# Moving the decode of most token mixing weights later, and centring the gate's rows on ScalarE

## The chip, the cores and the metric

One core of a Trainium2 chip. The metric is the device time of one execution in microseconds, as the median of several runs; the profile is of one further execution. The core's engines are TensorE (PE), VectorE (DVE), ScalarE (ACT), GpSimd (POOL) and SyncE (SP), each of which works through its own instructions in a fixed order and waits in that order; transfers are issued from SP's and GpSimd's queues.

## What is computed

Three layers follow one another, with a batch of 4, 768 tokens, 8 heads of 48 and a width of 384:

```python
f = 1.0 / (1.0 + np.exp(-f_logit))
for t in range(S):
    state = f[:, :, t, :, None] * state + np.einsum('bhd,bhe->bhde', k[:, :, t], v[:, :, t])
    y[:, :, t] = np.einsum('bhd,bhde->bhe', q[:, :, t], state)
...
u, v = (h[..., :d_ff // 2], h[..., d_ff // 2:])    # h = gelu(x @ w_in)
v_n = (v - mu) / np.sqrt(var + 1e-06) * g_ln
v_s = np.einsum('ts,bsd->btd', w_sg, v_n) + b_sg[None, :, None]
x = x + (u * v_s) @ w_out
...
zr, zi = x * np.cos(x @ w_theta), x * np.sin(x @ w_theta)
u = x + np.einsum('ts,bsd->btd', w_tok_r, zr) + np.einsum('ts,bsd->btd', w_tok_i, zi)
out = u + np.maximum(u @ w_ch, 0.0)
```

`v - mu` is the centring of the gate's rows; `w_tok_r` and `w_tok_i` are the token mixing weights. Weights come as 64-bit floats.

## The kernel before, in words

Every product is made of three matmuls (L782 to L784) from operands split into a high and a low part. A planner (`Plan`, L172) holds each operation with an engine, a duration, what it reads and writes, and a due time `vt`. It runs through time once, on each engine takes the ready operation with the earliest due time (pulled earlier where a reader's due time asks for it), and so writes one fixed order for each engine. What a due time does depends on the buffers too: an operation whose buffer is held is not ready.

The work comes in this order. Attention of batch 0 runs alone. Then block1 (L932, the second layer) of batches 0 to 3, each with attention of the next batch spread over it (24 attention units in all; each transposes keys, updates states and multiplies), so that the block1 of batch 3, the last, has none beside it. Then block2 (L968 and on, the third layer) of batch 3, then of 0, 1 and 2. In block1 each of six chunks of 128 tokens is multiplied by the gate's half of `w_in`, goes through Gelu on ScalarE with a row sum (L957), is centred on VectorE (L963 scales the sum to minus the mean, L964 adds it), squared with a row sum (L969), and scaled by GpSimd's power of the variance (L981, L989). `p3` (L831) mixes over tokens in two passes of 72 matmuls; each pass ends with the evacuation of four accumulations (L845, L850, then hi cast L791 and low half L792). `p4` adds the output product; the one of the second pass of tokens is left over for the block that follows. In block2, `theta` (L867) makes the cosines and sines for six chunks, then `p6` (L902) streams 24 tiles of mixing weights.

Each mixing tile (24 of 128x384) is decoded once and kept in DRAM: `load_f32` (L411) loads the raw 64-bit words on SP's queue, ScalarE takes a first pass (L431), VectorE four of bit work (L432 to L435); `load_split` (L437) adds the hi cast on ScalarE (L445) and the low half on VectorE (L446) into a buffer `wt`, and `decode` (L477) writes `wt` to DRAM on GpSimd's queue (L482). There are two `raw`, three `dt` and one `wt` buffer. `stream` (L484) reads the tiles back into five `st` buffers on SP's queue. `channel_weights` (L460) does the same for `w_theta` and `w_ch` in chunks, into `wmid`; `channel_load` (L470) brings them back into the place of `w_in`. Due times of decodes are set at the end of `body`, where `va` is the end of block1 of batch 0 and `pl.vt` that of block1 of batch 3, in the planner's time.

Of the kernel before, what the change touches and what calls it, by code (L numbers as in the profile page):

```python
# [12 lines left out]
AF = mybir.ActivationFunctionType  # L13
# [36 lines left out]
N_W = 1  # L50
N_DT = 3
N_RAW = 2
BG_FROM = 0.0
BG_TO = 80.0
N_MM = 4
GROUPS0 = [(p, p + 1) for p in range(NP)]
GROUPS1 = GROUPS0
# [265 lines left out]
def body(tc, ctx, att, qkv, flog, w_in, g_ln, w_sgT, b_sg, w_out, w_theta, w_rT, w_iT, w_ch, out):  # L323
# [84 lines left out]
    def a1(n):  # L408
        return 0.1 + n * 0.00081
# [67 lines left out]
    def decode(pl, g, i, vt):  # L477
        m, s, t = order[i]
        w = pl.buf(g.w32, [P, 2, TH], F32R)
        src = srcs[m][s * P : (s + 1) * P, t * TH : (t + 1) * TH]  # L480
        load_split(pl, g, w, lambda: (w.t[:, 0], w.t[:, 1]), src, vt, background=True)
        dma(pl, "POOL", P * 3072, lambda: nc.gpsimd.dma_start(scratch1[i], w.t.bitcast(F32)), [w], [g.scr1[i]], vt=vt)  # L482
# [105 lines left out]
    def unit(pl, g, b, hf, p, f, fb, seed, sb, be, bb, t, parts, xst, carry):  # L588
# [84 lines left out]
        def state(c):  # L673
            (s0, b0), (s1, b1) = S[c], S[c + 1]
            if hf == 0 and c == 0:
                pl.op("DVE", 0.117, lambda: V.tensor_copy(s1(), U(0)), r=[ps], w=[b1])
            elif c % 2 or c == 0:
                b1 = fulls[c // 2] if c % 2 else b1
                s1 = (lambda: st.t[:, 2 * NC2 + c // 2]) if c % 2 else s1
                pl.op("DVE", 0.117, lambda: V.tensor_add(s1(), s0(), U(c)), r=[ps, b0], w=[b1])  # L680
            else:
                be_ = be[:, c // 2 - 1 : c // 2]
                pl.op(
                    "DVE", 0.117,
                    lambda: V.scalar_tensor_tensor(s1(), st.t[:, 2 * NC2 + c // 2 - 1], be_, U(c), ALU.mult, ALU.add), r=[ps, fulls[c // 2 - 1], bb], w=[b1],  # L685
                )
            if c % 2:
                s2, b2 = S[c + 1]
                pl.op(
                    "ACT", 0.23, lambda: nc.scalar.activation(s2(), s1(), AF.Copy, scale=be[:, c // 2 : c // 2 + 1]), r=[bb, fulls[c // 2]], w=[b2]  # L690
                )
# [77 lines left out]
    def moe(pl, g, xst, get, wmid, out_b, pace, first=False):  # L769
# [162 lines left out]
        def block1(before, resplit, keep=None):  # L932
            xsplits((0,) if first else (0, 1))
            stat = pl.buf(g.stat, [P, 3, NS])
            sm, sv, sr = ([Buf(of=stat) for _ in range(NS)] for _ in range(3))
            vn = [pl.buf(g.ar[i], [P, 2, 3, DH], F32R) for i in range(2)]
            vnb = [[Buf(of=vn[s // 3]) for _ in range(2)] for s in range(NS)]
            vts = []

            def vtiles(s, c=slice(None)):  # L940
                return vnb[s], lambda: (vn[s // 3].t[:, 0, s % 3, c], vn[s // 3].t[:, 1, s % 3, c])

            for s in range(NS):
                if s == NC2:
                    before()
                    if first:
                        u0 = p2(0)
                        xsplits((1,))
                ps = pl.buf(g.mm, [P, 512])
                hf, c = s // NC2, slice((s % NC2) * P, (s % NC2 + 1) * P)  # L950
                for k in range(NK):
                    w = g.win[k][2:]
                    mm3(ps, xtiles(hf, k, c), (w, lambda k=k: (win[:, 0, k, DH:], win[:, 1, k, DH:])), k == 0, k == NK - 1, DH)
                vt = pl.buf(g.tmp, [P, DH])
                pl.op(
                    "ACT", a1(DH) + 0.05,
                    lambda ps=ps, vt=vt, s=s: A(vt.t, ps.t, AF.Gelu_apprx_tanh, accum_out=stat.t[:, 0, s : s + 1]),  # L957
                    [ps], [vt, sm[s]], table="G",
                )

                def centre(vt=vt, s=s):
                    m = stat.t[:, 0, s : s + 1]
                    V.tensor_scalar(m, m, -1.0 / DH, None, ALU.mult)  # L963
                    V.tensor_scalar(vt.t, vt.t, m, None, ALU.add)  # L964

                pl.op("DVE", 0.5, centre, [], [vt, sm[s]])
                pl.op(
                    "ACT", a1(DH) + 0.1,  # L968
                    lambda vt=vt, s=s: A(junk, vt.t, AF.Square, accum_out=stat.t[:, 1, s : s + 1]), [vt], [sv[s]],  # L969
                )  # L970
                vts.append(vt)
                if s % 3 == 2:
                    gs = slice(s - 2, s + 1)
                    pl.op(
                        "DVE", 0.07,
                        lambda gs=gs: V.tensor_scalar(stat.t[:, 2, gs], stat.t[:, 1, gs], 1.0 / DH, 1e-6, ALU.mult, ALU.add),
                        sv[gs], sr[gs],
                    )
                    pl.op(
                        "POOL", 0.8,  # L980
                        lambda gs=gs: nc.gpsimd.tensor_tensor(stat.t[:, 2, gs], stat.t[:, 2, gs], mhalf[:, gs], ALU.pow),  # L981
                        [], sr[gs],
                    )
                    for i in range(s - 2, s + 1):
                        hi, lo = vnb[i]
                        tl = vtiles(i)[1]
                        pl.op(
                            "ACT", a1(DH) + 0.1,
                            lambda i=i, tl=tl: nc.scalar.mul(tl()[0], vts[i].t, stat.t[:, 2, i : i + 1]), [vts[i], sr[i]], [hi],  # L989
                        )  # L990
                        pl.op(
                            "DVE", v1(DH),
                            lambda i=i, tl=tl: V.scalar_tensor_tensor(
                                tl()[1], vts[i].t, stat.t[:, 2, i : i + 1], tl()[0].bitcast(F32), ALU.mult, ALU.subtract
                            ),
                            [vts[i], sr[i], hi], [lo],
                        )

            if not first:
                u0 = p2(0)  # L1000
            g0 = p3(0, u0, vtiles)
            if first:
                weights_out(pl, g, pl.vt)
            u1 = p2(1)
            p4(0, g0, resplit, keep)
            g1 = p3(1, u1, vtiles)
            return lambda: p4(1, g1, resplit, keep)
# [26 lines left out]
    with tc.manual_schedule():  # L1034
# [27 lines left out]
        for b in range(B):  # L1062
# [5 lines left out]
                va = pl.vt  # L1068
            if b != last:
                x = spread(b + 1, v + (pl.vt - v) * (LATE / 100 if b == 0 else 0.0))  # L1070
        n = len(order) - 2 * NS
        for i in range(n):
            if i in (n // 3, 2 * n // 3):
                channel_weights(pl, g, i // (n // 3) - 1, va + (pl.vt - va) * (BG_FROM + (BG_TO - BG_FROM) * i / n) / 100)
            decode(pl, g, 2 * NS + i, va + (pl.vt - va) * (BG_FROM + (BG_TO - BG_FROM) * i / n) / 100)
        mids = [channel_load(pl, g, i, pl.vt - 8.0, i) for i in range(2)]
        for b in (last, *range(last)):
            if b != last:
                x = []
# [157 lines left out]
```

## Time and profile before

| what | value |
|---|---|
| median of 3 runs | 677.27 us (672.85 to 678.81) |
| the profiled execution's own time | 677.74 us |
| its span, first to last instruction | 676.0 us |
| mean granted TensorE clock | 0.975 |
| busy TensorE, VectorE | 616.3, 453.6 us |
| busy ScalarE, GpSimd | 342.3, 99.5 us |

Busy time is time in which at least one instruction of an engine runs. Matmuls overlap, so that a busy TensorE need not be at its peak; its granted clock is given as a share of the full 2.4 GHz.

### The profile page before, as it was taken

Reading aid. Unit: us, or ns where it says so; the run is one execution under the profiler, and the core shown is the slowest. Engines: PE = TensorE matmul, PEld = TensorE weight load, DVE = VectorE, ACT = ScalarE, POOL = GpSimd, SP = SyncE. Lnnn points to the kernel's source line nnn. Section 1 sums busy time; section 2 is a strip of 40 time slices with the busy share of each in tenths; the row PEclk is TensorE's granted clock in tenths of the full one; section 3 lists DMA queues with packets and bytes.
Section 4 is the critical chain, followed back from the end, with each engine's and each line's share of the span. In section 5 each row is a group of like instructions: output and inputs, shape, how many; then the busy total and the mean of one; then the engine's idle time right before and its main releaser. Section 6 shows DMA issues by size and latency. Waiting matters only on the chain.

```text
span 676.0 us, 15027 instructions
## 1 busy us (share of the span) xinstructions
PE 616.3 (91%) x5953; PEld 569.8 (84%) x5953; DVE 453.6 (67%) x1077; ACT 342.3 (51%) x728; POOL 99.5 (15%) x178
## 2 busy tenths in 40 slices
PE   8788688989999988988989999899999999999996
PEld 8667567778788876878878999799989998998995
DVE  6999778969999897889979333741482175148203
ACT  6658587646685665675536421740291055019200
POOL 2000222143241340341131100000000000000000
PEclk9899969999999998999999999999999999999998
DMA  9522836377578787477575455058628844860762
GB/s 331 190 84 74 285 120 217 120 264 270 170 252 248 245 258 270 147 245 250 173 264 212 144 190 182 23 165 253 207 77 277 252 154 156 252 219 25 250 194 76
DMA packets 49296, 131.50 MB, mean 195 GB/s; under 512 B 6816, under 2 KB 17248, under 8 KB 48960
## 3 DMA queue, kind: packets, MB, share of 16 engines
q1 hardware_dynamic: 38656, 88.95, 41.2%
q0 software_dynamic: 10560, 41.49, 17.7%
q8 instruction: 49, 0.80, 0.5%
q14 instruction: 31, 0.25, 0.1%
HBM read 100.93 MB, written 24.77 MB: 186 GB/s over the span
## 4 chain that ended last, share of the span: by engine, by line
PE 42%; DVE 23%; ACT 11%; DMA 11%; issue 9%; POOL 2%; SPq 0%; DVEq 0%; POOLq 0%; ACTq 0%
PE mm L782 14%; PE mm L783 13%; PE mm L784 13%; DMA f<-in_flog 3%; DMA scratch<-wt 3%; DMA dt<-in_w_sgT 2%; DMA raw<-in_w_iT 2%; DVE s L680 2%; DVE dt L434 1%; DVE dt L435 1%; ACT ar L791 1%; DVE s L685 1%; DVE am L660 1%; POOL xst L755 1%; DVE tmp L845 1%
## 5 line engine op out<-in xcount | busy, mean ns | idle before, releaser
L782 PE MATMUL mm<-st,ar 128*128 128x384 f32 x480 | 164.9, 344 | 2.5 <-DMA st<-scratch 2.4
L783 PE MATMUL mm<-st,ar 128*128 128x384 f32 x480 | 161.4, 336 | 0.0
L784 PE MATMUL mm<-st,ar 128*128 128x384 f32 x480 | 161.4, 336 | 0.0
L801 ACT CAST x<-xst 128x384 fp32r<-128x384 f32 x72 | 36.9, 513 | 146.8 <-DVE xst L806 126.7
L806 DVE TENSOR_TENSOR xst<-xst,mm 128x384 f32<-128x384 f32 x48 | 25.7, 552 | 115.4 <-PE mm L784 115.4
L782 PEld LDWEIGHTS mm<-st,ar 128*128 128x128 f32 x480 | 90.9, 189 | 5.1 <-DMA st<-scratch 2.7
L783 PEld LDWEIGHTS mm<-st,ar 128*128 128x128 f32 x480 | 91.0, 190 | 0.1
L784 PEld LDWEIGHTS mm<-st,ar 128*128 128x128 f32 x480 | 90.8, 189 | 0.0
L782 PE MATMUL mm<-win,x 128*128 128x512 f32 (+1 forms) x144 | 56.6, 393 | 7.4 <-DVE tmp L845 3.7
L782 PE MATMUL mm<-x,win 128*128 128x384 f32 x168 | 58.4, 348 | 0.0
L784 PE MATMUL mm<-win,x 128*128 128x512 f32 (+1 forms) x144 | 54.1, 376 | 3.0 <-DVE x L802 3.0
L791 ACT CAST ar<-tmp 128x384 fp32r<-128x384 f32 x80 | 37.7, 509 | 37.7 <-DVE tmp L850 36.8
L784 PE MATMUL mm<-x,win 128*128 128x384 f32 x168 | 56.3, 335 | 0.0
L783 PE MATMUL mm<-x,win 128*128 128x384 f32 x168 | 56.2, 335 | 0.0
L783 PE MATMUL mm<-win,x 128*128 128x512 f32 (+1 forms) x144 | 53.5, 372 | 0.1
L802 DVE TENSOR_TENSOR x<-xst,x 128x384 fp32r<-128x384 f32 x72 | 37.8, 553 | 7.7 <-ACT x L801 6.4
L792 DVE TENSOR_TENSOR ar<-tmp,ar 128x384 fp32r<-128x384 f32 x80 | 41.0, 553 | 0.7 <-ACT ar L791 0.2
L782 PE MATMUL mm<-ar,wout 128*128 128x384 f32 x96 | 35.6, 371 | 4.2 <-DVE tmp L845 2.4
L782 PEld LDWEIGHTS mm<-win,x 128*128 128x128 f32 x144 | 27.8, 193 | 13.1 <-DVE tmp L845 5.4
L784 PE MATMUL mm<-ar,wout 128*128 128x384 f32 x96 | 33.3, 347 | 1.1 <-DVE wout L446 1.1
L755 POOL DMA_DIRECT2D xst<-y x60 | 30.7, 516 | 20.8 <-ACT y L732 10.9
L783 PE MATMUL mm<-ar,wout 128*128 128x384 f32 x96 | 33.4, 348 | 0.4 <-DVE ar L792 0.4
(146 smaller groups left out, 1227.2 us busy)
## 6 DMA issues: line engine op xcount, KB each, us to landing
st<-scratch SPq DMA_DIRECT2D x132, 384.0 KB, 3.8
qkv<-in_qkv POOLq DMA_DIRECT2D x24, 536.0 KB, 6.1
scratch<-wt POOLq DMA_DIRECT2D x24, 384.0 KB, 4.1
raw<-in_w_rT SPq DMA_DIRECT2D x12, 384.0 KB, 5.7
raw<-in_w_iT SPq DMA_DIRECT2D x12, 384.0 KB, 3.9
f<-in_flog POOLq DMA_DIRECT2D x6, 768.0 KB, 4.8
scratch<-st POOLq DMA_DIRECT2D x12, 384.0 KB, 6.7
out<-xst SPq DMA_DIRECT2D x24, 192.0 KB, 2.0
```

The lines of the kernel that those rows point to most:

```text
L434: op(v1(n), lambda: V.scalar_tensor_tensor(iget(), bits()[1], -0x40000000, iget(), ALU.bitwise_and, ALU.bitwise_or))
L435: op(v1(n), lambda: V.scalar_tensor_tensor(iget(), bits()[0], 29, iget(), ALU.logical_shift_right, ALU.bitwise_or))
L680: pl.op("DVE", 0.117, lambda: V.tensor_add(s1(), s0(), U(c)), r=[ps, b0], w=[b1])
L755: lambda r0=r0, n=n, kc=kc, o=64 * j + off: q[yq].dma_start(xst.t[r0 : r0 + n, kc], y.t[o : o + n].rearrange("p i a t -> p (i a t)")),
L782: nc.tensor.matmul(o, h0, h1, start=start, stop=False)
L783: nc.tensor.matmul(o, h0, l1, start=False, stop=False)
L784: nc.tensor.matmul(o, l0, h1, start=False, stop=stop)
L791: pl.op("ACT", a1(n), lambda: nc.scalar.copy(tiles()[0], src.t[:, :n]), [src], [hi])
L792: pl.op("DVE", v1(n), lambda: V.tensor_sub(tiles()[1], src.t[:, :n], tiles()[0].bitcast(F32)), [src, hi], [lo])
L801: pl.op("ACT", a1(TH), lambda: nc.scalar.copy(X[hf][:, 0, k], T()), [src], [hi])
L802: pl.op("DVE", v1(TH), lambda: V.tensor_sub(X[hf][:, 1, k], T(), X[hf][:, 0, k].bitcast(F32)), [src, hi], [lo])
L806: pl.op("DVE", v1(TH), lambda: V.tensor_add(T(), T(), ps.t[:, :TH]), [ps], [xst[hf].parts[k]])
```

## The change

Three things are edited: the due times of the decodes (8 spread over the time after block1 of batch 0, 16 from 6 us ahead of the planned end of the last block1 in steps of 3.3 us; `w_theta` at 0.4 of the span, `w_ch` and its load after the end); centring, where GpSimd makes minus the mean and ScalarE adds it; and the planner's durations of the state updates. From the planner's numbers at the top on, line numbers of the new kernel are one higher up to the centring (L431 is L432, L845 is L846).

```diff
-BG_FROM = 0.0
-BG_TO = 80.0
+N_EARLY = 8
+LATE_AT = -6.0
+LATE_STEP = 3.3
...
-                pl.op("DVE", 0.117, lambda: V.tensor_copy(s1(), U(0)), r=[ps], w=[b1])
+                pl.op("DVE", 0.2, lambda: V.tensor_copy(s1(), U(0)), r=[ps], w=[b1])
...
-                pl.op("DVE", 0.117, lambda: V.tensor_add(s1(), s0(), U(c)), r=[ps, b0], w=[b1])
+                pl.op("DVE", 0.16, lambda: V.tensor_add(s1(), s0(), U(c)), r=[ps, b0], w=[b1])
...
-                    "DVE", 0.117,
+                    "DVE", 0.19,
...
-                def centre(vt=vt, s=s):
-                    m = stat.t[:, 0, s : s + 1]
-                    V.tensor_scalar(m, m, -1.0 / DH, None, ALU.mult)
-                    V.tensor_scalar(vt.t, vt.t, m, None, ALU.add)
-
-                pl.op("DVE", 0.5, centre, [], [vt, sm[s]])
+                m = lambda s=s: stat.t[:, 0, s : s + 1]
+                pl.op("POOL", 0.15, lambda m=m: nc.gpsimd.tensor_scalar(m(), m(), -1.0 / DH, None, ALU.mult), w=[sm[s]])
+                pl.op("ACT", a1(DH), lambda m=m, vt=vt: A(vt.t, vt.t, AF.Identity, bias=m()), [sm[s]], [vt])
...
-        n = len(order) - 2 * NS
-        for i in range(n):
-            if i in (n // 3, 2 * n // 3):
-                channel_weights(pl, g, i // (n // 3) - 1, va + (pl.vt - va) * (BG_FROM + (BG_TO - BG_FROM) * i / n) / 100)
-            decode(pl, g, 2 * NS + i, va + (pl.vt - va) * (BG_FROM + (BG_TO - BG_FROM) * i / n) / 100)
-        mids = [channel_load(pl, g, i, pl.vt - 8.0, i) for i in range(2)]
+        span = pl.vt - va
+        channel_weights(pl, g, 0, va + 0.4 * span)
+        for i in range(len(order) - 2 * NS):
+            early = va + span * (0.1 + 0.8 * i / N_EARLY)
+            decode(pl, g, 2 * NS + i, early if i < N_EARLY else pl.vt + LATE_AT + (i - N_EARLY) * LATE_STEP)
+        channel_weights(pl, g, 1, pl.vt + 20.0)
+        mids = [channel_load(pl, g, i, pl.vt + (-8.0, 40.0)[i], i) for i in range(2)]
```

VectorE's order in the block1 of batch 1, where the second pass of `p3` is evacuated (L845 is one accumulation, `dt` a tile being decoded, `qkv` and `seed` attention of batch 3), before:

```order
L845 SCALAR_TENSOR_TENSOR tmp_3427<-mm_96,gcol,bbc 128x384
L432 TENSOR_SCALAR dt_3429<-dt_3429 128x384
L433 TENSOR_SCALAR dt_3429<-dt_3429 128x384
L434 SCALAR_TENSOR_TENSOR dt_3429<-raw_3356,dt_3429 128x384
L850 TENSOR_TENSOR tmp_3427<-tmp_3427,u_2984 128x384
L845 SCALAR_TENSOR_TENSOR tmp_3450<-mm_97,gcol,bbc 128x384
L435 SCALAR_TENSOR_TENSOR dt_3429<-raw_3356,dt_3429 128x384
L850 TENSOR_TENSOR tmp_3450<-tmp_3450,u_3001 128x384
L845 SCALAR_TENSOR_TENSOR tmp_3464<-mm_98,gcol,bbc 128x384
```

The same place in the changed kernel (lines one higher):

```order
L846 SCALAR_TENSOR_TENSOR tmp_3359<-mm_96,gcol,bbc 128x384
L803 TENSOR_TENSOR x_90<-xst_0_3050,x_90 128x384
L851 TENSOR_TENSOR tmp_3359<-tmp_3359,u_2947 128x384
L447 TENSOR_TENSOR wt_3302<-dt_3143,wt_3302 128x384
L803 TENSOR_TENSOR x_90<-xst_0_3050,x_90 128x384
L793 TENSOR_TENSOR ar_0_3381<-tmp_3359,ar_0_3381 128x384
L612 TENSOR_TENSOR qkv_3300<-qkv_3300,seed_3018 128x384
L613 TENSOR_TENSOR seed_3018<-seed_3018,f_3034 128x384
L846 SCALAR_TENSOR_TENSOR tmp_3397<-mm_97,gcol,bbc 128x384
L851 TENSOR_TENSOR tmp_3397<-tmp_3397,u_2972 128x384
L846 SCALAR_TENSOR_TENSOR tmp_3429<-mm_98,gcol,bbc 128x384
```

The bit work between the evacuations is gone; one low half and attention's multiplications stand there.

ScalarE's order in the last block1, from the Gelus of its second pass (`u`) to the hi casts of the second evacuation (`ar`) and theta's first Copy, before:

```order
L827 ACTIVATE u_5079<-mm_96 128x384
L827 ACTIVATE u_5096<-mm_97 128x384
L801 CAST x_89<-xst_1_3733 128x384 x3
L791 CAST ar_0_5232<-tmp_5212 128x384
L791 CAST ar_0_5232<-tmp_5217 128x384
L791 CAST ar_0_5232<-tmp_5222 128x384
L791 CAST ar_0_5232<-tmp_5239 128x384
L887 ACTIVATE tmp_5263<-mm_97 128x384
```

The same place in the changed kernel:

```order
L828 ACTIVATE u_5023<-mm_95 128x384
L446 CAST wt_5038<-dt_4862 128x384
L802 CAST x_89<-xst_1_3673 128x384
L432 ACTIVATE dt_5048<-raw_4931 128x384
L802 CAST x_89<-xst_1_3673 128x384 x2
L446 CAST wt_5093<-dt_4907 128x384
L432 ACTIVATE dt_5105<-raw_5029 128x384
L446 CAST wt_5139<-dt_5004 128x384
L432 ACTIVATE dt_5150<-raw_5085 128x384
L446 CAST wt_5191<-dt_5048 128x384
L792 CAST ar_0_5198<-tmp_5176 128x384
L792 CAST ar_0_5198<-tmp_5181 128x384
```

Four hi casts of decoded tiles and three first passes of further ones now stand ahead of the evacuation's casts.

## Rows read from the trace of the kernel before

**Rows 1.** Busy time by stretch: PE, PEld, DVE, ACT, POOL, PEclk, DMA share, GB/s
```profile
100.60:158.20 57.60, 49.61 (x794) 43.32 (x785) 49.56 (x119) 38.01 (x71) 19.25 (x35) 0.97 0.61 206
158.20:180.70 22.50, 21.53 (x236) 17.89 (x234) 20.73 (x52) 13.43 (x32) 6.52 (x12) 1.00 0.58 191
180.70:243.80 63.10, 58.71 (x853) 52.60 (x844) 59.98 (x142) 46.32 (x92) 21.24 (x36) 1.00 0.77 246
243.80:278.80 35.00, 29.48 (x268) 25.45 (x262) 28.94 (x70) 18.17 (x41) 7.72 (x14) 0.90 0.65 226
278.80:344.10 65.30, 61.11 (x850) 54.16 (x851) 60.45 (x150) 40.17 (x86) 19.50 (x35) 1.00 0.67 219
344.10:394.10 50.00, 46.82 (x262) 42.80 (x256) 28.30 (x67) 21.11 (x51) 9.73 (x17) 0.97 0.62 213
394.10:419.10 25.00, 25.00 (x146) 25.00 (x145) 9.23 (x19) 5.12 (x11) 0.00 (x0) 1.00 0.59 189
419.10:442.20 23.10, 20.17 (x117) 18.68 (x115) 18.26 (x38) 15.95 (x33) 0.00 (x0) 1.00 0.11 35
```

**Rows 2.** What ended TensorE's idle time, 100 to 344 us: total, times, longest
```profile
PE at L703 <- DVE s L680: 6.6, 7, 1.7
PE at L639 <- ACT kt L631: 5.8, 4, 2.8
PE mm L782 <- DVE tmp L845: 3.1, 2, 2.4
...
PE mm L782 <- DMA st<-scratch: 2.4, 1, 2.4
```

**Rows 3.** Groups by shape, the decode: busy us, mean ns | idle before
```profile
L434 DVE SCALAR_TENSOR_TENSOR dt<-raw,dt 128x384 int32<-128x384 int32 x30 | 16.7, 557 | 0.7
...
L435 DVE SCALAR_TENSOR_TENSOR dt<-raw,dt 128x384 int32<-128x384 int32 x30 | 16.7, 556 | 0.6
...
L433 DVE TENSOR_SCALAR dt<-dt 128x384 int32<-128x384 int32 x34 | 13.6, 404 | 0.8
...
L446 DVE TENSOR_TENSOR wt<-dt,wt 128x384 fp32r<-128x384 f32 x24 | 13.2, 552 | 2.0 <-ACT wt L445 2.0
...
L445 ACT CAST wt<-dt 128x384 fp32r<-128x384 f32 x24 | 12.2, 509 | 15.1 <-DMA scratch<-wt 8.6 <-DVE dt L435 6.5
L432 DVE TENSOR_SCALAR dt<-dt 128x384 f32<-128x384 f32 x34 | 12.0, 356 | 1.3 <-ACT dt L431 1.3
```

**Rows 4.** Groups by shape, centring and its nearest kin
```profile
L989 ACT ACTIVATE ar<-tmp,stat 128x512 fp32r<-128x512 f32 x24 | 15.8, 714 | 5.1 <-POOL stat L981 5.1
...
L964 DVE TENSOR_SCALAR tmp<-tmp,stat 128x512 f32<-128x512 f32 x24 | 11.7, 487 | 0.8
...
L963 DVE TENSOR_SCALAR stat<-stat 128x1 f32<-128x1 f32 x24 | 3.6, 148 | 3.7 <-ACT tmp L957 3.7
...
L1041 POOL COPY gate<-win 128x1 f32<-128x1 f32 x1 | 0.6, 642 | 7.0 <-DVE win L446 7.0
```

**Rows 5.** VectorE in order of time, two operations back to back
```profile
251.19 0.55 DVE L613 SCALAR_TENSOR_TENSOR qkv<-seed,qkv 128x384 f32<-128x384 f32 x1
251.66 0.55 DVE L614 TENSOR_TENSOR qkv<-qkv,f 128x384 f32<-128x384 f32 x1
```

**Rows 6.** ScalarE in order of time, 376 to 383 us; landing times of wt
```profile
376.46 0.50 ACT L445 CAST wt<-dt 128x384 fp32r<-128x384 f32 x1
...
379.63 0.49 ACT L827 ACTIVATE u<-mm 128x384 f32<-128x384 f32 x1 [0.46 <-PE mm L784]
...
382.95 0.51 ACT L445 CAST wt<-dt 128x384 fp32r<-128x384 f32 x1 [0.63 <-DMA scratch<-wt]
...
DMA to landing us min/median/max: 2.6/4.1/7.1
```

**Rows 7.** ScalarE in order of time, hi casts of the last block1's two evacuations
```profile
396.79 0.51 ACT L791 CAST ar<-tmp 128x384 fp32r<-128x384 f32 x1 [12.55 <-DVE tmp L850]
...
421.30 0.93 ACT L791 CAST ar<-tmp 128x384 fp32r<-128x384 f32 x2 [12.02 <-DVE tmp L850]
```

## The prediction, made before the result was known

> **What bounds the kernel now.** I read busy time by stretch, then who waited for whom, then single stretches in order of time. The reader is to see three regimes. From 442 us on come the rest of the first block2 and three more, which the change hardly touches. From 344 to 442 us the last block1 and the first theta stage run: TensorE is full from 394 to 419, and VectorE is busy for only 28.30 + 9.23 + 18.26 = 55.8 of 98.1 us there. Between 100.6 and 344.1 us attention of the next batch runs beside block1, and there VectorE is the full engine: 49.56 + 20.73 + 59.98 + 28.94 + 60.45 = 219.7 of 243.5 us, 90% [rows 1]. TensorE's idle time in those five stretches is 7.99 + 0.97 + 4.39 + 5.52 + 4.19 = 23.1 us, and it ran at a granted clock of 0.97 in the first and 0.90 in the fourth, so that another 57.6 x 0.03 + 35 x 0.10 = 5.2 us went to the lower of its two levels (1.2 instead of 2.4 GHz), which follows on such gaps. So 28.3 us is all that TensorE could give back in these stretches. Of the waits that end its gaps there, the most are for VectorE (state updates at L680, evacuations at L845: 9.7 us), then for ScalarE's transposed keys (5.8), once for a transfer (2.4) [rows 2].
>
> **The change part by part.**
>
> *Decoding moved later.* One decode is on VectorE 0.356 + 0.404 + 0.557 + 0.556 us of bit work and 0.552 of low half, 2.43 us, and on ScalarE a first pass and a hi cast of 0.509 [rows 3]. By the order, up to the mask multiply of the last attention unit VectorE runs 20 instead of 29 of the bit chains and 29 instead of 40 of the 384-wide low halves: 9 x 1.873 + 11 x 0.552 = 22.9 us less. The name of the change promises 16 tiles in block2; the order shows something else. The single wt buffer and the due times of its readers pull most of them forward: 10 hi casts stand ahead of the end of attention (18 before), 8 between there and the first evacuation of the last block1, 4 between its two evacuations, where VectorE had time, and 2 in theta, with the three chunks of w_ch.
>
> *Centring moved.* Each of 24 gate rows gives up 0.148 + 0.487 us on VectorE, and 18 of them lie in the attention stretches or ahead of them: 11.4 us [rows 4]. ScalarE takes a 512-wide pass with a per-row operand; the nearest row is its scaling at 0.714 us, so 18 x 0.714 = 12.9 us more, against 11 hi casts less (11 x 0.509 = 5.6) and 9 first passes. ScalarE is busy 38.01 + 13.43 + 46.32 + 18.17 + 40.17 = 156 of 243.5 us there and has room [rows 1]. GpSimd gets 24 one-column multiplies. Bounds for one: 0, if other queued work of ScalarE covers the wait, and 0.642 us, the one-column copy, GpSimd's nearest operation of that size; I take 0, since ScalarE has that room, and the other end is rival D's [rows 4].
>
> *What the relief is worth.* VectorE is freed of 22.9 + 11.4 = 34.3 us by durations. Back to back they start 0.47 us apart although each lasts 0.55, so some 29 us of its time [rows 5]. It was 90% full, TensorE has 23.1 us idle and 5.2 lost on the clock. Ends: 4 us (only the gaps that evacuations at L845 end, 3.1, and the clock after the longest of them) and 28.3 (all). I take half, **-14.2 us**: the listed waits name VectorE for 9.7 us and others for 8.2 [rows 2], and once VectorE has slack the next late ones are keys from ScalarE (5.8) and the transfers of weights and forget logits. At the end of block1 of batch 1 bits of a decode stand between the evacuations of one pass; there lie the longest wait for an evacuation, 2.4 us, and the low clock of the fourth stretch. The order now has other work there, attention's. The stretch from 0 to 100.6 changes little: no tile of the mixing weights stood there; I take 0 and +-3.
>
> *State costs in the planner* (0.117 to 0.16 to 0.20) are numbers of the planner, not instructions; they change which of two ready operations goes first. 0, +-2.
>
> *The new wait.* In the last block1 hi casts on ScalarE now stand in a row. Each needs the one wt buffer, free only when the write to DRAM of the tile before has landed. Cast to cast took 6.49 us where nothing else held it [rows 6]. By the pieces (0.51 cast, 0.55 low half, handovers of 0.1 to 0.25, 4.1 us median from issue to landing) it is 5.8 [rows 3, 6]. Four casts stand ahead of the first evacuation's hi casts, which began at 396.79, and four more ahead of the next, at 421.30 [rows 7]. The first of the four follows a Gelu that ended at 380.1; three cycles later it is 397.5 (at 5.8) or 399.6 (at 6.49), so the evacuation's casts start at 398.0 or 400.1, 1.2 to 3.3 us late. The second run starts once the low half has got past the evacuation (some 9 us later) and takes three more cycles: 424.5 or 428.6 against 421.30, **3.2 to 7.3 us late, I take 5**. Queued behind these casts on ScalarE are the splits that p4(1) reads and all of theta; TensorE waits for both. Before, ScalarE was idle there for 12.55 and 12.02 us, and that was the cover.
>
> *In theta* (419.1 to 442.2) VectorE gets three low halves, three of each first pair of bit operations and two of each second pair ahead of its last multiply: 3 x 0.552 + 3 x 0.760 + 2 x 1.113 = 6.2 us [rows 3]. It had 23.1 - 18.26 = 4.8 us idle there [rows 1]. Ends 1.4 (all idle time used) and 6.2; idle time there is handovers with ScalarE, so I take **+3**.
>
> *Transfers.* Each moved tile takes along its load on SP's queue and its write on GpSimd's. On SP loads of the streamed tiles stand behind raw loads that wait for a decode, but in the order the sixth tile of a pass is the first with such a wait ahead of it, and five buffers cover it: 0, at most the 2.4 us that one late tile cost before [rows 2]. The 12 matmuls that now come after attention cost the same in either place. w_ch is stored in theta, and p7 reads it only after both passes of `p6`: 0.
>
> Sum: 677.74 - 14.2 + 5 + 3 = 671.5 for the profiled execution, which lies 0.47 over the median of the runs, so **671**.
>
> **Rivals.**
> *A, the relief is worth all of it:* gaps and low clock both go, and the casts go at the fast pace: 677.3 - 28.3 + 3.2 + 1.4 = 653.6. For it: VectorE loses about as much as TensorE could give back. Against it: keys, transfers and the release chain of states stay.
> *B, VectorE was full but not late:* TensorE was busy 49.61 + 21.53 + 58.71 + 29.48 + 61.11 = 220.4 of 243.5 us, as full as VectorE; if its gaps are handovers, only 4 us go: 677.3 - 4 + 8 = 681.
> *C, slower, the one wt buffer holds ScalarE:* with writes that land in 7.1 us, the longest seen, a cycle is 5.8 + 3.0 = 8.8 us. The delay grows by about (7.3 - 3.2) / 0.69 = 5.9 us for each us of cycle, so theta starts 3.2 + 17.7 = 21 us late: 677.3 - 14.2 + 21 + 6.2 = 690. The gain is gone from a cycle of about 7.2 us, and the loss over 1% from 8.3. For it: reads of streamed tiles share the DMA engines there (0.59 busy). Against it: the cast at 382.95 waited only 0.63 us.
> *D, centring is dearer where it goes:* ScalarE stands in line for GpSimd, which stands in line for transfers; 18 x (0.714 + 0.642 - 0.635) = 13 us, if all of it lands on the path: 677.3 - 14.2 + 13 + 8 = 684. The Trainium skill (ScalarE: Activation LUTs, Rules for kernel authors) says so in general: adds and multiplies belong on VectorE, not ScalarE. By that rule the pass is dearer, and the rows agree (0.714 against 0.487); it speaks for D only where ScalarE is late, which its 64% here does not show.
>
> **How the numbers follow.** Forecast 0.43 (its own range, from 5 us either way of the relief and the ends of the casts, 661 to 680), A 0.20, B 0.18, C 0.12, D 0.07. One per cent, 6.8 us, is about what a measurement of this kernel can tell from no change. Faster by over 1% is below 670.5: half of the forecast, A, little of B and D: 0.22 + 0.20 + 0.03 + 0.01 = 0.46. Slower, above 684.0: C, half of D, some of B and of the forecast: 0.12 + 0.04 + 0.03 + 0.02 = 0.21. Within 1%: 0.33. The range leaves out the ends of A and of C: 655 to 686.
>
> **What would show it.** Right: VectorE's busy time between the first and last attention unit falls by about 30 us, TensorE's idle time there to some 10, and the last attention output comes near 330 us. ScalarE's idle time before hi casts of wt, ended by writes of wt, is several us at the end of both evacuations of the last block1, and theta's first Copy starts about 5 us later after the attention's end than before. Wrong: the stretch from 100 to 344 keeps its length while VectorE is idler (B); ScalarE waits for GpSimd's one-column multiply by more than 5 us in all (D); casts of wt 8 us apart (C).

## The result, and the profile after

The changed kernel takes 669.1 us (median of nine runs, 665.2 to 673.68), the kernel before 676.52 in the nine beside it: a ratio of 0.9904 with an interval of 0.988 to 0.9929, so 1% faster. The forecast was 671.0.

The head of its page:

```profile
span 671.8 us, 15019 instructions
...
PE 615.1 (92%) x5963; PEld 566.7 (84%) x5963; DVE 445.8 (66%) x1029; ACT 355.9 (53%) x752; POOL 107.9 (16%) x202
```

The profiled execution is the longest of the nine (673.68), so its stages show 4.1 us of the 7.4 between the medians. Each is bounded by an event that both programs have: the 8th, 16th, 24th and last copies of the attention output (L732, now L733), the first evacuation (L845, L846) of either pass of the last block1, and the first theta Copy of the first and second block2 (L887, L888). All times are us.

| kernel | to 8th | to 16th | to 24th | to last | to evacuation 1 | to evacuation 2 | to theta | first block2 | rest |
|---|---|---|---|---|---|---|---|---|---|
| before | 66.2 | 92.7 | 86.0 | 103.4 | 45.8 | 25.0 | 4.7 | 66.1 | 186.2 |
| changed | 65.0 | 89.6 | 85.4 | 89.1 | 53.1 | 27.3 | 4.7 | 71.1 | 186.5 |

The same stretches by engine, first of the kernel before (8th to last copy, to the first evacuation, to theta, the first block2; columns as in [rows 1]):

```profile
66.20:348.30 282.10, 249.91 (x3215) 218.91 (x3214) 246.97 (x588) 179.65 (x366) 84.76 (x146) 0.96 0.66 220
348.30:394.10 45.80, 42.62 (x216) 38.68 (x215) 26.89 (x64) 21.08 (x51) 7.79 (x13) 0.96 0.59 201
394.10:423.80 29.70, 29.70 (x174) 29.66 (x173) 13.90 (x28) 7.03 (x15) 0.00 (x0) 1.00 0.58 185
423.80:489.90 66.10, 63.17 (x364) 61.69 (x363) 29.64 (x60) 24.46 (x51) 0.00 (x0) 1.00 0.51 159
```

and of the changed kernel:

```profile
65.00:329.20 264.20, 240.14 (x3174) 209.10 (x3173) 219.00 (x502) 176.97 (x357) 85.72 (x152) 0.97 0.62 203
329.20:382.30 53.10, 48.93 (x253) 45.62 (x252) 30.31 (x65) 27.25 (x61) 9.84 (x20) 0.97 0.65 214
382.30:414.30 32.00, 29.04 (x165) 28.36 (x166) 22.86 (x49) 11.16 (x25) 2.23 (x4) 1.00 0.72 246
414.30:485.30 71.00, 64.03 (x363) 61.50 (x362) 37.53 (x78) 27.73 (x59) 2.15 (x4) 1.00 0.59 203
```

The reader takes length minus busy TensorE. Up to the last copy it falls from 32.2 to 24.1 us. Behind it, it rises in each of the three: 3.2 to 4.2, 0 to 3.0, 2.9 to 7.0, in all 8.0 us given back. The second row must be read with its count: 253 matmuls now stand there in place of 216, so of its 7.3 us more 6.3 are TensorE's own work that lay ahead of the last copy before. At equal work the stretch up to the last copy is thus 17.9 - 6.3 = 11.6 us shorter, 8.1 of it idle time; the rest goes with the higher granted clock (0.97 for 0.96). VectorE has 28.0 us less to do there.

What ended TensorE's idle time from 100.6 us to the last copy, which answers [rows 2]:

```profile
PE at L628 <- ACT y L733: 6.7, 5, 2.2
PE at L704 <- DVE s L681: 2.1, 5, 0.7
PE at L640 <- ACT kt L632: 1.5, 4, 0.7
PE at L704 <- DVE s L686: 1.4, 3, 0.7
...
PE mm L783 <- DVE tmp L846: 1.0, 4, 0.4
```

Two further lines of the view of before belong beside them:

```profile
PE at L703 <- DVE s L685: 2.7, 5, 1.0
...
PE at L627 <- ACT y L732: 0.6, 1, 0.6
```

Waits for state updates (L680 and L685, now L681 and L686) fell from 6.6 + 2.7 = 9.3 to 3.5 us, for transposed keys from 5.8 to 1.5, for the evacuation from 3.1 to 1.0. One came in their place: 6.7 us for ScalarE's copies of the attention output, 0.6 before.

The groups that answer [rows 3, 4]:

```profile
L964 ACT ACTIVATE tmp<-tmp,stat 128x512 f32<-128x512 f32 x24 | 16.5, 719 | 0.5 <-POOL stat L963 0.5
...
L446 ACT CAST wt<-dt 128x384 fp32r<-128x384 f32 x24 | 12.3, 511 | 35.7 <-DMA scratch<-wt 32.7 <-DVE dt L436 2.9
...
L963 POOL TENSOR_SCALAR stat<-stat 128x1 f32<-128x1 f32 x24 | 8.4, 353 | 59.8 <-ACT tmp L958 59.7
```

ScalarE's centring takes 0.719 us, as its scaling did. It sat idle for GpSimd's multiply for 0.5 us in all. The hi casts of tiles show the new wait: 32.7 us for the write of `wt`, 8.6 before. Nearly all of it lies behind 329 us:

```profile
ACT wt L446 <- DMA scratch<-wt: 30.2, 9, 5.2
```

ScalarE in order of time there, hi casts of tiles (L446), of the evacuations (L792) and a split of `x` (L802), which answers [rows 6, 7]:

```profile
370.85 0.52 ACT L446 CAST wt<-dt 128x384 fp32r<-128x384 f32 x1 [0.42 <-DMA scratch<-wt]
...
378.67 0.51 ACT L446 CAST wt<-dt 128x384 fp32r<-128x384 f32 x1 [5.23 <-DMA scratch<-wt]
...
384.86 0.51 ACT L446 CAST wt<-dt 128x384 fp32r<-128x384 f32 x1 [4.50 <-DMA scratch<-wt]
385.28 0.51 ACT L792 CAST ar<-tmp 128x384 fp32r<-128x384 f32 x1
...
395.44 0.51 ACT L446 CAST wt<-dt 128x384 fp32r<-128x384 f32 x1 [4.42 <-DMA scratch<-wt]
395.86 0.51 ACT L802 CAST x<-xst 128x384 fp32r<-128x384 f32 x1
...
405.92 0.51 ACT L446 CAST wt<-dt 128x384 fp32r<-128x384 f32 x1 [3.94 <-DMA scratch<-wt]
...
412.13 0.51 ACT L446 CAST wt<-dt 128x384 fp32r<-128x384 f32 x1 [4.52 <-DMA scratch<-wt]
412.55 1.75 ACT L792 CAST ar<-tmp 128x384 fp32r<-128x384 f32 x4
```

From 378 us on the casts of tiles, all but one (at 400.25), stand 4 to 5 us at their buffer, with the evacuation's casts right behind. These start 3.0 us after their evacuation (382.27 and 409.54 us), against 2.7 and 2.2 before: little late. What TensorE felt is the tile's cast at 395.44 and the split of `x` right behind it. VectorE stood 3.34 us for the cast, and its low halves of the tile and of `x` are queued ahead of the output sums (L807) that free TensorE's accumulators:

```profile
398.05 0.44 PE L783 MATMUL mm<-st,ar 128*128 128x384 f32 x1 [1.32 <-DVE xst L807]
...
399.85 0.44 PE L783 MATMUL mm<-st,ar 128*128 128x384 f32 x1 [1.01 <-DVE xst L807]
```

And in the first block2 TensorE waited twice for transfers:

```profile
PE mm L783 <- DMA st<-scratch: 1.6, 1, 1.6
PE mm L783 <- DMA win<-scratch: 1.3, 1, 1.3
```

The second is the product with `w_ch`: its store took 8.8 us and its load 6.4.

### The profile page after: what moved, and what is told of

Same layout as the page of the kernel before. It is cut to its first block, busy times and chain, and to the rows that moved or that the text cites. A ratio compares the mean times of both kernels' runs of the same rounds, so it can differ in the third digit from the quotient of the medians.

```text
span 671.8 us, 15019 instructions
## 1 busy us (share of the span) xinstructions
PE 615.1 (92%) x5963; PEld 566.7 (84%) x5963; DVE 445.8 (66%) x1029; ACT 355.9 (53%) x752; POOL 107.9 (16%) x202
## 3 DMA queue, kind: packets, MB, share of 16 engines
q0 software_dynamic: 10560, 41.49, 17.8%
## 4 chain that ended last, share of the span: by engine, by line
PE 31%; DVE 24%; ACT 19%; DMA 14%; issue 9%; POOL 2%; SPq 0%; DVEq 0%; POOLq 0%; ACTq 0%
PE mm L783 10%; PE mm L785 10%; PE mm L784 10%; DMA raw<-in_w_iT 3%; DMA scratch<-wt 3%; DVE dt L435 2%; DMA xst<-y 2%; DMA dt<-in_w_sgT 2%; ACT ar L792 2%; DVE s L681 2%; DVE dt L436 2%; DVE ar L793 2%; ACT tmp L964 1%; ACT junk L967 1%; ACT tmp L958 1%
## 5 line engine op out<-in xcount | busy, mean ns | idle before, releaser
L802 ACT CAST x<-xst 128x384 fp32r<-128x384 f32 x72 | 36.7, 512 | 150.5 <-DVE xst L807 126.6
L807 DVE TENSOR_TENSOR xst<-xst,mm 128x384 f32<-128x384 f32 x48 | 25.8, 551 | 109.9 <-PE mm L785 109.8
L783 PE MATMUL mm<-x,win 128*128 128x384 f32 x168 | 58.9, 351 | 3.1 <-DVE tmp L846 1.8
L792 ACT CAST ar<-tmp 128x384 fp32r<-128x384 f32 x80 | 37.7, 508 | 12.0 <-DVE tmp L851 11.1
L783 PEld LDWEIGHTS mm<-win,x 128*128 128x128 f32 x144 | 27.4, 190 | 14.2 <-DVE tmp L846 5.3
L783 PE MATMUL mm<-ar,wout 128*128 128x384 f32 x96 | 34.6, 360 | 2.0 <-DVE tmp L898 1.8
L783 PEld LDWEIGHTS mm<-x,win 128*128 128x128 f32 x168 | 31.8, 189 | 5.1 <-DVE tmp L846 2.4
L785 PEld LDWEIGHTS mm<-win,x 128*128 128x128 f32 x144 | 27.6, 191 | 7.4 <-DVE x L803 4.4
```

The source lines that it names most:

```text
L783: nc.tensor.matmul(o, h0, h1, start=start, stop=False)
L785: nc.tensor.matmul(o, l0, h1, start=False, stop=stop)
L792: pl.op("ACT", a1(n), lambda: nc.scalar.copy(tiles()[0], src.t[:, :n]), [src], [hi])
L802: pl.op("ACT", a1(TH), lambda: nc.scalar.copy(X[hf][:, 0, k], T()), [src], [hi])
L807: pl.op("DVE", v1(TH), lambda: V.tensor_add(T(), T(), ps.t[:, :TH]), [ps], [xst[hf].parts[k]])
```

## The experiments

Theory 1, from the prediction: VectorE's freed time makes the attention stretches shorter, and the one wt buffer gives part of it back. Its rivals stand in the expectations. Every kernel was timed beside the kernel before.

| kernel | centring on | decodes | state costs | tile buffers | median us | ratio to before (interval) |
|---|---|---|---|---|---|---|
| e1 | ScalarE | early | old | wt | 675.98 | 0.9997 (0.9968 to 1.0026) |
| e5 | VectorE | early | new | wt | 676.59 | 0.9999 (0.9969 to 1.003) |
| e8 | VectorE | early | measured | wt | 678.32 | 1.0051 (1.0019 to 1.0082) |
| e2 | VectorE | late | new | wt | 666.93 | 0.9858 (0.9823 to 0.9893) |
| e3 | ScalarE | late | old | wt | 681.81 | 1.0079 (1.0047 to 1.0111) |
| changed | ScalarE | late | new | wt | 669.1 | 0.9904 (0.988 to 0.9929) |
| e6 | ScalarE | late | measured | wt | 674.54 | 0.9992 (0.9955 to 1.0029) |
| e4 | ScalarE | late | new | wt, spare | 664.06 | 0.9839 (0.979 to 0.9888) |
| e10 | ScalarE | late | old | wt, spare | 674.55 | 0.9991 (0.9967 to 1.0015) |
| e9 | ScalarE | late | measured | wt, spare | 667.51 | 0.9872 (0.9833 to 0.9911) |
| e7 | VectorE | late | new | wt, spare | 664.65 | 0.9808 (0.9757 to 0.986) |
| e11 | VectorE | late | new | wt, one spare | 663.82 | 0.9819 (0.9787 to 0.9851) |
| e12 | VectorE | late | new | wt, spare from the 13th | 662.81 | 0.9818 (0.9784 to 0.9853) |

Stages of all of them:

| kernel | to 8th | to 16th | to 24th | to last | to evacuation 1 | to evacuation 2 | to theta | first block2 | rest |
|---|---|---|---|---|---|---|---|---|---|
| e1 | 66.7 | 92.2 | 88.4 | 98.9 | 43.0 | 25.0 | 4.7 | 66.9 | 186.2 |
| e5 | 65.2 | 88.6 | 85.8 | 107.6 | 45.2 | 25.0 | 4.7 | 67.4 | 186.2 |
| e8 | 63.7 | 90.9 | 91.1 | 103.0 | 45.7 | 25.0 | 4.7 | 66.0 | 186.5 |
| e2 | 64.2 | 88.8 | 86.4 | 88.6 | 47.4 | 27.7 | 4.7 | 71.7 | 186.0 |
| e3 | 67.1 | 91.7 | 87.6 | 90.4 | 52.6 | 27.7 | 4.7 | 71.1 | 186.1 |
| e6 | 65.6 | 87.9 | 86.0 | 89.2 | 53.9 | 28.7 | 6.0 | 71.6 | 186.4 |
| e4 | 65.4 | 87.0 | 85.1 | 89.4 | 52.5 | 24.6 | 4.7 | 66.0 | 186.0 |
| e10 | 67.0 | 94.3 | 86.8 | 94.0 | 49.9 | 24.6 | 4.7 | 66.1 | 186.6 |
| e9 | 65.4 | 89.3 | 86.9 | 91.1 | 51.8 | 24.5 | 4.7 | 66.1 | 186.2 |
| e7 | 65.3 | 88.0 | 85.7 | 90.8 | 53.3 | 24.5 | 4.7 | 66.1 | 186.4 |
| e11 | 65.2 | 88.9 | 85.2 | 88.6 | 51.3 | 24.5 | 4.7 | 66.0 | 186.2 |
| e12 | 63.9 | 88.9 | 85.8 | 89.8 | 49.4 | 24.7 | 4.7 | 66.1 | 186.2 |

A profile is one execution; stages of two kernels are compared here only where they differ by more than the 3 us or so that these executions lie from their kernel's median (4.6 us in the changed kernel), or where several kernels agree.

### e1 and e2: the two moves apart

e1, the kernel before with

```diff
-                pl.op("DVE", 0.5, centre, [], [vt, sm[s]])
+                pl.op("POOL", 0.15, lambda m=m: nc.gpsimd.tensor_scalar(m(), m(), -1.0 / DH, None, ALU.mult), w=[sm[s]])
+                pl.op("ACT", a1(DH), lambda m=m, vt=vt: A(vt.t, vt.t, AF.Identity, bias=m()), [sm[s]], [vt])
```

> The kernel before with the centring alone moved (GpSimd scales, ScalarE adds); decodes stay where they were. Theory 1 (what counts is VectorE's time freed ahead of the end of attention, and it is worth the same whichever part frees it): centring is 11.4 of the 34.3 us freed, the changed kernel's attention stretches are 10.7 us shorter, so 11.4 / 34.3 x 10.7 = 3.6 us off, with nothing given back later: 676.5 - 3.6 = about 673. Theory 2 (centring on ScalarE costs there what it frees on VectorE, since TensorE now waits 6.7 us for ScalarE's copies of the attention output): 676 to 680. Theory 3 (centring is the whole gain, the late decodes give back all that they bring): 669.

e2, the changed kernel with these lines the other way round.

> The changed kernel with the centring back on VectorE; late decodes and state costs stay. Theory 1: 22.9 of the 34.3 us freed, 7.1 us off in the attention stretches, and the 7.6 us given back behind them stay: 677. Theory 2: the attention stretches keep all of their 10.7 us or gain more, since ScalarE is relieved: 669 or less, and TensorE's wait for copies of the attention output falls from 6.7 to under 2 us. Theory 3: 676.5.

Measured: 675.98 and 666.93. Theory 2 has both times, e1's at its edge. Of its reason only half holds: in e2 TensorE's wait for the copies of the attention output fell from 6.7 to 4.0 us, not below 2. So the 11.4 us of VectorE's time that centring frees are worth nothing that these runs can tell. Beside late decodes the two ratios lie 0.5% apart against the move, but their intervals overlap, so that a cost is not shown; e4 and e7 show none either. Theory 3 falls.

### e3: the planner's numbers back

```diff
-                pl.op("DVE", 0.2, lambda: V.tensor_copy(s1(), U(0)), r=[ps], w=[b1])
+                pl.op("DVE", 0.117, lambda: V.tensor_copy(s1(), U(0)), r=[ps], w=[b1])
...
-                pl.op("DVE", 0.16, lambda: V.tensor_add(s1(), s0(), U(c)), r=[ps, b0], w=[b1])
+                pl.op("DVE", 0.117, lambda: V.tensor_add(s1(), s0(), U(c)), r=[ps, b0], w=[b1])
...
-                    "DVE", 0.19,
+                    "DVE", 0.117,
```

> The changed kernel with the planner's old durations for the state updates (0.117 everywhere); centring and late decodes as changed. Theory 1: the numbers change no instruction, so within 2 us of the changed kernel's 669. Theory 4 (the gain in the attention stretches is the better order of the states: TensorE waited 9.3 us for them before and 3.5 after): 674 to 677, with the waits for states back at 9 us.

Measured: 681.81, slower than the kernel before. Neither theory allowed for that. Three numbers that change no instruction are worth 1.0079 against 0.9904, 12.7 us between the medians, more than the whole result. In the profiles the changed kernel is 7.0 us shorter, 6.3 of them ahead of the 24th copy. What ended TensorE's idle time up to the 24th copy, in the kernel before:

```profile
PE at L703 <- DVE s L680: 9.9, 9, 2.0
PE at L703 <- DVE s L685: 6.3, 6, 1.6
PE at L639 <- ACT kt L631: 5.0, 5, 2.8
```

in e3:

```profile
PE at L704 <- DVE s L681: 6.6, 9, 2.0
PE at L704 <- DVE s L686: 5.7, 6, 1.6
PE at L640 <- ACT kt L632: 5.5, 9, 1.8
```

and in the changed kernel:

```profile
PE at L628 <- ACT y L733: 6.7, 5, 2.2
PE at L704 <- DVE s L686: 4.2, 6, 1.0
...
PE at L704 <- DVE s L681: 3.7, 6, 1.1
...
PE at L640 <- ACT kt L632: 1.1, 4, 0.4
```

States and keys together held TensorE for 21.2, 17.8 and 9.0 us. The copies of the attention output rise from 3.1 us in e3 to 6.7 in the changed kernel and take back part; 5.2 of the 6.3 us are these three waits. That with 0.117 the planner puts what reads a state close behind the update that makes it (201 and 262 ns on the chip), so that TensorE gets there first and stands, is read from how the planner works.

The other kernels bear the gain out. In those with 0.117 (before, e1, e3, e10) TensorE stands 16.6 to 21.2 us for states and keys, and they come to the 24th copy at 244.9 to 248.1 us; in the seven with the changed numbers (changed, e2, e4, e5, e7, e11, e12) it stands 9.0 to 14.7 us, and they come at 237.6 to 240.0. The waits do not tell everything: in e8 it stands 8.8 us, and e8 comes at 245.7, but has some 90 matmuls more ahead of that copy.

### e4: a spare buffer for late tiles

```diff
-        w = pl.buf(g.w32, [P, 2, TH], F32R)
+        w = pl.buf(g.qkv if i >= 2 * NS + 10 else g.w32, [P, 2, TH], F32R)
```

> The changed kernel, in which decoded tiles from the eleventh on (those of the last block1 and theta) go to the four qkv buffers, free once attention is done, in place of the one wt buffer; nothing else is edited. Theory 1 (the 7.6 us given back behind attention come from ScalarE standing at the one wt buffer ahead of the evacuations and splits): its 30.2 us of waits for the write of wt fall to under 5, TensorE's idle time in the two stretches up to theta falls by 3 to 4 us, theta gets fewer low halves: 669 - 4 to 5 = 664.5. Theory 5 (they come from the decode work itself, which VectorE and ScalarE now do there with or without a wait): 669 or more.

Measured: 664.06. By stages, in the order of those above from the last copy on:

```profile
326.90:379.40 52.50, 49.13 (x253) 45.62 (x252) 36.82 (x78) 29.82 (x67) 13.81 (x27) 0.97 0.79 271
379.40:408.70 29.30, 28.62 (x165) 28.35 (x166) 22.04 (x48) 10.24 (x22) 1.08 (x2) 1.00 0.72 248
408.70:474.80 66.10, 63.27 (x365) 61.74 (x364) 29.98 (x62) 24.45 (x52) 0.00 (x0) 1.00 0.57 179
```

Idle TensorE is 3.4, 0.7 and 2.8 us, in all 6.9, against 14.1 in the changed kernel and 6.1 in the one before; of the 8.0 us given back 0.8 are left. No wait of a cast for a write is left there, with eleven tiles cast behind the last copy (fourteen in the changed kernel). ScalarE at the place of the fence above:

```profile
390.97 0.50 ACT L802 CAST x<-xst 128x384 fp32r<-128x384 f32 x1
392.82 0.52 ACT L802 CAST x<-xst 128x384 fp32r<-128x384 f32 x1 [1.35 <-DVE xst L807]
...
397.12 0.50 ACT L802 CAST x<-xst 128x384 fp32r<-128x384 f32 x1
...
406.23 0.93 ACT L792 CAST ar<-tmp 128x384 fp32r<-128x384 f32 x2 [6.14 <-DVE tmp L851]
```

The splits wait for what makes their data, and the evacuation's casts for VectorE. Theory 1 holds behind attention, and theory 5 falls: up to theta VectorE is busy longer than in the changed kernel (58.9 against 53.2 us), and TensorE still idles less. With the tiles ready earlier, `w_ch` is too: the waits for streamed tiles and for `win` in the first block2 are gone.

### e5 and e8: the planner's numbers alone

e5 is the kernel before with 0.2, 0.16 and 0.19, the three lines of the change; e8 has 0.25, 0.20 and 0.26 there.

> The kernel before with only the planner's three durations for state updates changed (0.117 to 0.2, 0.16 and 0.19); no instruction is added or taken away. Theory 4 (the durations are what the change lives by: with the old ones the changed kernel took 681.8, with the new ones 669.1): the same share off the kernel before, 676.7 x 669.1 / 681.8 = 664, with the eighth unit of attention near 64 us and the sixteenth near 154 in place of 66 and 159. Theory 6 (the new durations only help where the late decodes have made room on VectorE): 672 to 677, the sixteenth unit near 159.

> The kernel before with the planner's durations for state updates at what the profile shows (0.25, 0.20, 0.26) and nothing else. Theory 4a: as e5 or less, 664 or below. Theory 4b: between 664 and 680, not ordered by how true the numbers are.

Measured: 676.59 and 678.32. Both theories of e5 were half right: it reaches the 16th copy at 153.8 us as theory 4 wants and ends as theory 6 wants. e8 came out as theory 4b has it. Of the 5.3 us that e5 gains up to the 24th copy 4.2 go in the next stage, which takes 107.6 us, and most of the rest in the first block2. In that stage ScalarE, with the first pass of a tile ahead of the passes that make attention's `seed`, stood for raw words:

```profile
244.09 0.55 ACT L431 ACTIVATE dt<-raw 128x384 f32<-128x384 f32 x1 [3.60 <-DMA raw<-in_w_rT]
```

VectorE's order has 15 operations of decodes ahead of the attention unit's multiplications (L611 to L614) and between them:

```profile
244.67 0.36 DVE L432 TENSOR_SCALAR dt<-dt 128x384 f32<-128x384 f32 x1 [2.70 <-ACT dt L431]
...
253.67 0.56 DVE L435 SCALAR_TENSOR_TENSOR dt<-raw,dt 128x384 int32<-128x384 int32 x1
254.15 0.55 DVE L613 SCALAR_TENSOR_TENSOR qkv<-seed,qkv 128x384 f32<-128x384 f32 x1
```

The first and the last row of decode lie 9 us apart. VectorE has no gap between them, 6.9 us of the time up to `qkv` are decodes, and `qkv` comes only then. TensorE, whose releaser the view does not name, goes on 0.1 us after it:

```profile
254.80 0.87 PE L627 MATMUL at<-ident,qkv 128*128 128x128 f32 x3 [7.59 <-issue]
```

e8 has the same queue in the same place, and there the view names the releaser:

```profile
PE at L627 <- DVE qkv L613: 6.0, 1, 6.0
```

In e2 these decodes stand elsewhere, and the stage takes 88.6 us. So the numbers alone gain nothing (0.9999): what they save ahead of the 24th copy goes to decodes behind it. Late decodes without the numbers gain nothing either (1.0079 beside 0.9997 for e1): e3 is 6.3 us faster than the kernel before between the 24th copy and the first evacuation and gives back 7.6 behind it. Both together bring 1.4% (e2). Late decodes with 0.117 and centring on VectorE were not run.

### e6, e9 and e10: the same numbers with one buffer and with spare ones

e6 is the changed kernel with the durations of the profile (0.25, 0.20, 0.26); e9 is e4 with them, e10 is e4 with 0.117.

> The changed kernel with the planner's durations for state updates at what the profile shows (copy 0.25, add 0.20, multiply and add 0.26) in place of 0.2, 0.16 and 0.19. Theory 4a (the order is better the nearer the planner's durations are to the chip's): 669 or less. Theory 4b (the order that came out with these three numbers is a lucky one; any other set moves it by several us either way): 672 or more, with waits for states no shorter than the changed kernel's 3.5 us.

> e4 (spare buffers) with the planner's state durations at the profile's values (0.25, 0.20, 0.26). e6, the same numbers with the one wt buffer, reached the 24th unit of attention at 239.5 us, no later than the changed kernel (240.0), and lost its 5 us behind attention (first to second evacuation 28.7 against 27.3 us, to theta 6.0 against 4.7). Theory 8 (the numbers shift work by a little, and the one wt buffer makes a loss of it): with spare buffers the loss is gone, 664 as e4. Theory 4b (a lucky order): 669 or more, the loss spread over other stages.

> e4 (spare buffers) with the old state durations (0.117). Theory 9 (the new durations are worth some 5 to 6 us in the stages up to the 24th unit, whatever follows: e5 reached it at 239.6, the changed kernel at 240.0, the kernels with the old ones at 244.9 to 247.3): 24th unit near 246, the stages after it as in e4, 664 + 6 = 670. Theory 8: the one wt buffer made the difference between the changed kernel and e3: within 2 us of e4's 664.

Measured: 674.54, 667.51 and 674.55. The numbers called measured did not make a faster order, and neither e6 nor e8 bears theory 4a out. But they are the chip's for two of the three operations only. Their 0.25 for the copy is a mean that one copy of 1.015 us pulls up, in the kernel before:

```profile
L676 DVE COPY s<-at x16: 181/201/1015, 13.3 to 297.8; 128x48 f32<-128x48 f32 x16
```

The median is 0.201 us, which is the changed kernel's number; 0.20, 0.20 and 0.26 together were not run. e6 has the time of theory 4b, but the shorter waits for states (2.2 us from 100 us on) against it, and loses behind attention: from the first evacuation to the end of the first block2 it takes 28.7 + 6.0 + 71.6 = 106.3 us, the changed kernel 103.1 and e4 95.3. With spare buffers that is gone (95.3 in e9), as theory 8 says, but e9 is still 3.5 us slower than e4, with overlapping intervals. e10 comes to its 24th copy at 248.1 us, later than theory 9's 246, and ends 10.5 us behind e4. So what the changed numbers gain on 0.117 lies ahead of the 24th copy with either buffer (6.3 us from e3 to the changed kernel, 10.5 from e10 to e4), and the spare buffers' gain behind attention with any numbers: e3 to e10, changed to e4, e6 to e9 and e2 to e7 give 0.9%, 0.7%, 1.2% and 0.5%, the first and the third with intervals apart.

### e7, e11 and e12: towards a faster kernel

e7 is e4 with centring on VectorE. e11 is e7 but gives every second late tile `seed`'s place in the stead of a `qkv` buffer, and e12 is e7 from the thirteenth tile on:

```diff
-        w = pl.buf(g.w32, [P, 2, TH], F32R)
+        w = pl.buf(g.seed if i >= 2 * NS + 10 and i % 2 else g.w32, [P, 2, TH], F32R)
```

> The changed kernel with the spare buffers of e4 and with centring back on VectorE. Theory 2 (centring on ScalarE costs some 2 us, as e2 against the changed kernel has it, 0.46%): 664.1 - 2 to 3 = 661.5. Theory 7 (e2's gain came from shorter queues on ScalarE ahead of the one wt buffer, which the spare buffers already give): 664.

> As e7 (centring on VectorE, spare buffers for the late tiles), but only every second late tile goes to a spare buffer (seed's place, free once attention is done), the others to wt: two buffers in all. Theory 10 (e7 lost 6 us ahead of the first evacuation of the last block1 against e2, 53.4 to 47.5 us from the last attention output, because five buffers let ScalarE and VectorE take decodes ahead of the gate's rows: VectorE 41.9 us busy there against 34.5, a wait of TensorE for L846 of 3.1 us with a granted clock of 0.94): with two buffers that wait falls under 2 us while the wait at the evacuations stays gone: 659 to 662. Rival: two buffers wait like one, ScalarE's waits for the write over 15 us: 666 as e2.

> As e7, but the spare buffers take the tiles from the thirteenth on. By the order, eleven in place of fourteen hi casts of tiles stand ahead of the last attention output, the rest behind it. Theory 10: VectorE has less decoding in the third attention stage, more just behind it: within 2 us of e7's 664.6. Theory 4b (any change of the order moves the time by several us): more than 3 us off in either direction.

Measured: 664.65, 663.82 and 662.81. Theory 7 rather than 2 for e7: where ScalarE no longer stands at a buffer, these runs tell no difference between the engines that centre. e11 missed its range, since TensorE's longest wait for L846 stayed at 2.2 us; so theory 10's reason for e7's longer stretch is not shown. But two buffers do what five do. e12 came out as theory 10 has it. All four kernels with new numbers and spare buffers lie within 2 us and beat the one before; of their intervals only e4's touches the changed kernel's. e12's is the lowest median, 1.8% below the kernel before.

## Why the prediction came out right

*The bound.* VectorE's busy time up to the last copy fell by 28.0 us where about 30 were forecast, and the last copy came at 329.2 us for "near 330". This was read rightly, though 6.3 us of TensorE's work had moved behind it.

*The relief of -14.2 us.* The stretch up to the last copy became 11.6 us shorter at equal work, and the first 66 us 1.2 shorter. The size is near, the reason is half of it. Up to the first evacuation, where both kernels have done the same products, the changed kernel is 11.8 us ahead. Of these 4.9 lie ahead of the 24th copy, where the planner's numbers work, and 7.0 between that copy and the evacuation (149.2 to 142.2 us), where VectorE was relieved. There the ten kernels with late decodes take 136.0 to 144.1 us, those with early ones and centring on VectorE 148.7 to 152.7 (before, e5, e8), and e1, with centring moved alone, 141.8: either move gives VectorE enough slack there, and the second adds nothing. So relief is not proportional to the time freed, as theory 1 has it. That is near rival B's reading (full, but not late), which the forecast gave 0.18. e1 shows it by one profile alone, 2.3 us below its median, and e1's median is that of the kernel before.

*The state costs at "0, +-2".* This is the step that failed. "Numbers of the planner, not instructions; they change which of two ready operations goes first" is true, and beside late decodes it is worth 1.75% (e3 to the changed kernel), up to the 24th copy above all. [Rows 2] had named it: 6.6 us of waits for states at L680, the largest entry, which the forecast put down to VectorE being full; it left out the 2.7 us at L685. A state update that the planner holds for 0.117 us and that takes 201 to 262 ns would leave such a wait also on an idle engine. That the sum came out is luck in part: by the profiles the relief brought 7.0 us for 14.2, the numbers 4.9 for 0, and 7.6 came back behind the first evacuation for the 8 of the next two terms.

*The new wait, +5.* TensorE's idle time from the last copy to theta rose by 4.0 us. The mechanism is shown by e4 and its rows; the place was off. The casts of the evacuations came under 1 us later after their evacuation, not 1.2 to 3.3 and 3.2 to 7.3, and the delay that rows show went through the splits of `x`, which the forecast had named with theta. From cast to cast it took 7.8 and 6.2 us ahead of the first evacuation's casts (370.85, 378.67, 384.86), 4.8, 5.7 and 6.2 ahead of the second's (from 395.44), against the forecast's 5.8 to 6.49 and rival C's 8.8.

*Theta, +3, and transfers, 0.* The first block2 took 5.0 us more, of them 4.0 idle. In theta itself it was 1.9 for 3 (21.8 against 19.9 us from the first to the sixth Copy). 2.9 were the waits for a streamed tile and for `w_ch`, each costed at 0 (the tile with 2.4 as its other end). "p7 reads it only after both passes of `p6`" left out that store and load of `w_ch` take 15.2 us. Both waits lie behind theta, in the rest of the first block2, which by the forecast the change hardly touches.

*Centring.* GpSimd's multiply as a wait of ScalarE at 0 was right, 0.5 us in all. The pass costs 0.719 us on ScalarE for 0.487 on VectorE. The Trainium skill (ScalarE: Activation LUTs, Rules for kernel authors) wants adds on VectorE, and the two rows agree. In the kernel's time these runs do not show it: 0.5% with overlapping intervals (e2 against the changed kernel), nothing alone (e1) or with spare buffers. Rival D's 684 is far off.

What stays open: why one set of three numbers orders the program better than another. Three sets spread the changed kernel over 1.75% and e4 over 1.5%; the middle one is the fastest both times (beside e9 with overlapping intervals), though two of its numbers, 0.16 and 0.19, are shorter than the chip's 0.20 and 0.26. Open too is what late decodes are worth with 0.117 and centring on VectorE.

## What to carry to other kernels

Where a planner writes the order, its durations are part of the change: time them alone and with the rest, before a gain is credited to the work that was moved. Time that is freed on an engine which is 90% busy does not come back in proportion: where VectorE was relieved, the first move took what there was, and the second nothing. Work that is moved into idle time must find not only an engine there but a free buffer: with one buffer that is written to memory in each round, ScalarE stood for 30 us and held what was queued behind it, and buffers that had come free elsewhere in the program were worth 0.5 to 1.2%.

## What was not expected of the hardware

Three transfers of `y` (72, 48 and 24 KB) that were issued in a row in e5 took 9.5 to 10.2 us to land, against a median of 4.3 there. They come just ahead of TensorE's gap of 7.6 us, but VectorE had no gap for them, so that they are not shown to be its cause. GpSimd's one-column multiply ran in a median of 0.228 us, a third of the one-column copy that the forecast took as its bound, though one took 2.372.
